# Agent attention and two feed-forward layers: the second layer moved one block further behind the first, and its weights decoded later

## The chip, the cores and the metric

The kernel runs on one core of a Trainium2 chip. The metric is the device time of one execution in microseconds (us); three runs of the kernel before gave a median of 1066.42 us. The engines are named as the profile names them: PE is TensorE, PEld its weight loads, ACT is ScalarE, DVE is VectorE, POOL is GpSimd, and SP is the engine whose queue issues all DMAs here.

## The reference

12480 tokens of width 128 attend through 49 agents, and the result passes two feed-forward layers with 2048 hidden columns. In the reference's words, cut to what is computed:

```
a2k = softmax(scale * agents @ k.T);  agent_v = a2k @ v          # 49 x 128
q2a = softmax(scale * q @ agents.T);  x = q2a @ agent_v          # 12480 x 128
h = x @ w_in1;  g = where(h >= 1, h, where(h <= -1, 0, (h + 1)**2 / 4));  y = g @ w_out1
h = y @ w_in2;  g = s * max(h, 0)**2 + b;                         out = g @ w_out2
```

The four weight matrices arrive as 64-bit floats and are decoded on the chip into a high and a low part (`fp32r`, a rounded fp32 that PE multiplies in one go).

## The kernel before, in words

**Before the first product.** All 13 groups of keys and then 13 groups of values are loaded by SP. PE forms the scores of the agents against the keys (`ks`), DVE finds their maxima, ACT takes exponentials (line 557, token `E`), PE turns them round (`st`), ACT or DVE copies them (`tok`, tokens `V`), and PE sums the values (`av`, tokens `a`). DVE divides (`avn`, token `n`), PE turns the result (`at`, token `T`), ACT and DVE split it (`avh`, `avl`, tokens `H`, `L`). Then PE multiplies it into the first layer's input weights (`aw`, tokens `W0` to `W3`), ACT rounds the product to `awh` (tokens `F`) and DVE keeps the rest in `awl` (tokens `G`). From then on the first layer works on the 49 attention weights of a token instead of its 128 values.

**Weights.** Each matrix comes in two pieces of 1 MB: B is `w_in1`, C is `w_out1`, D is `w_in2`, A is `w_out2`. A piece is decoded in eight steps, numbered 0 to 7; steps 1, 2 and 5 are on ACT (lines 381, 384, 399), the others on DVE (lines 376, 394, 389, 402, 407). `D0.1` is step 1 of piece D0. Three buffers hold raw pieces, so a load waits until step 7 of an earlier piece has freed one. The order of the loads on SP is the string `LOADS`; the order of everything else before the steady state is two strings of tokens, `SEQ` and `RAMP`, in which each engine runs its own tokens in the order written.

**Steps.** The tokens are cut into 25 blocks: one of 256, 23 of 512, one of 448. A block has eight steps of two hidden chunks each; step n belongs to block n // 8. In the first layer a step is `H` (products into PSUM), `R` and `S` (ACT: relu, square), `M` (DVE: cap), then a split into `gh` (token `c` on DVE or `g` on ACT) and `gl` (token `L`, DVE), and `O` (products into `y`). The first 12 steps are short: they skip the split, and `O` multiplies the fp32 values with fp32 weights (`w32`, built by tokens `U` from the decoded C). When a block of `y` is complete, ACT and DVE split it into `yh` and `yl`, and the second layer runs the same kind of step on it, in small letters: `h`, `r`, square, `G` or `c`, `l`, `o`. Three PSUM buffers of two banks take the results of `H`, `h`, the scores and the turned pieces.

**Steady state.** After the string `RAMP`, the function `steady` writes the steps two at a time by the table `PAIR`: step n of the first layer beside step n - D of the second. The lag D is one block and three steps, 11 steps. When the first layer is through, `TAIL` writes the rest of the second.

**Attention of the later blocks.** Blocks 3 and later get their attention weights in pairs of blocks. Pair v loads its queries, PE forms scores, DVE turns them into the tile `turned` (line 269), softmax follows there, DVE turns the packed result back into `turned` (line 284), and 32 DMAs (line 297) move it from `turned` into `pt` and `px`, from where `H` reads. Pair v is asked for at step 8 b - 17, where b is its first block; pair 0 at step 15.

Of the kernel before, what the change touches and what calls it, by code (L numbers as in the profile page):

```python
# [8 lines left out]
F32 = mybir.dt.float32  # L9
F32R = mybir.dt.float32r  # L10
# [8 lines left out]
def kernel(  # L19
# [18 lines left out]
    P = 128  # L38
# [11 lines left out]

    GR, XB, UB, WB, KV = 4, 3, 3, 2, 7
    WARM, CD = 10, 1
    PAT1, PAT2, TL = "11111101000001", "11011101", 11

# [6 lines left out]


    SEQ = (
# [8 lines left out]
    )  # L74
    VDVE = (0, 3, 4, 7, 8, 12)
    LOADS = (
        "k0 B0 k1 k2 k3 B1 k4 k5 k6 k7 k8 k12 k9 k10 k11 C0 v0 q0 D0 v1 C1 v2 v3 v4 v5 D1 v6 v7 v9 q1 v8 v10 v11 "
        "v12 A0 q2 A1"
    )
    RAMP = (  # L80
# [5 lines left out]
    )  # L86
    WORD = "B0 B1 C0 D0 C1 D1 A0 A1".split()
    NR, FP = 14, 12
    PAIR = {
        "PE": "H0 O0 o0 h0 O1 h1 o1 q1".split(),  # L90
        "ACT": "t0 R0 S0 G0 R1 S1 Y0 r0 Y1 t1 G1 r1".split(),
# [123 lines left out]
    def q_transpose(t):  # L215
        if t >= NB:
            return
        fill(len(fillers))
        w = blocks[t][1]
        tp = ps_h(f"tp{t}")[:, 0, :]  # L220
        for i, c0 in enumerate(subs(t)):
            nc.tensor.matmul(
                out=tp[:, c0:c0 + P], lhsT=ptok[t % NPT][:, i, :], rhs=ident_r,
                start=True, stop=True,
            )
        pt = pt_t[t] = ptp.tile([P, TB], F32R, tag="pt", name=f"pt{t}")
        if t >= QB:
            px = px_t[t] = late.tile([P, TB], F32R, tag="px", name=f"px{t}", bufs=3)

        def spread():  # L230
            nc.scalar.activation(out=pt[:, :w], in_=tp[:, :w], func=ACTF.Copy)
            if t < QB:
                return
            src = pt.bitcast(F32)
            for g in range(P // RG):
                nc.sync.dma_start(out=px.bitcast(F32)[g * RG:g * RG + XL, :w], in_=src[XN:NA, :w])

        qev.append(spread)
# [183 lines left out]
        )  # L422

    def sums_copy():
        cs.append(late.tile([P, TB], F32, tag="px", name="csum", bufs=3))
        nc.scalar.activation(out=cs[1], in_=cs[0], func=ACTF.Copy)

    def sums_turn():
# [28 lines left out]
    def agents_values(pro, dec, wi1h, wi1l):  # L457
# [157 lines left out]
            nc.vector.tensor_tensor(out=avl, in0=at[0], in1=avh.bitcast(F32), op=ALU.subtract)  # L615

        def weights(i):
            aw[i] = ps_h(f"aw{i}")[:, 0, :]
            ops = [(avh, wi1h), (avh, wi1l), (avl, wi1h)]
            for m, (a, w) in enumerate(ops):  # L620
                nc.tensor.matmul(
                    out=aw[i], lhsT=a, rhs=w[:, i * TB:(i + 1) * TB], start=(m == 0), stop=(m == len(ops) - 1)
                )
# [56 lines left out]
    JP = KF // 2  # L680
    NS = NB * JP
    D1, D2 = 2, 2
    D = JP + D1 + DX
    hp, gx, gh, gl = {}, {}, {}, {}
    y_ps, y_hl, o_ps = {}, {}, {}

# [17 lines left out]

    def fill_rows():

        extra["m"] = late.tile([P, DFF], F32R, name="awm")
        extra["x"] = late.tile([P, DFF // 4], F32R, name="awx")
        m, x, h, l = (w.bitcast(F32) for w in (extra["m"], extra["x"], awh, awl))
        for i, r in enumerate((0, LO)):  # L710
            nc.sync.dma_start(out=m[i * NA:(i + 1) * NA], in_=h[r:r + NA])
        nc.sync.dma_start(out=m[2 * NA:P], in_=l[0:XN])
        for g in range(P // RG):
            nc.sync.dma_start(
                out=x[g * RG:g * RG + XL].rearrange("p (q m) -> p q m", m=P),
                in_=l[XN:NA].rearrange("p (q g m) -> p q g m", g=4, m=P)[:, :, g, :],
            )
# [21 lines left out]
        return layer == 1 and n < FP  # L739

    def ring(kind, layer, n, dtype, bufs):
        pool = late if layer == 1 else extra["late2"]
        t = pool.tile([P, 2 * TB], dtype, tag=f"{kind}{layer}", name=f"{kind}{layer}_{n}", bufs=bufs)
        return t.rearrange("p (b n) -> p b n", b=2)

# [39 lines left out]

    def GH(layer, n):
        if layer == 1:
            return PAT1[n] if n < len(PAT1) else "0"
        return PAT2[n % len(PAT2)] if n < NS - TL else "0"

    def last_step(first):
# [40 lines left out]
    def evac(layer, part):  # L832
        if layer not in done:
            return
        t = done[layer]
        t0, w = blocks[t]
        o = o_ps[layer]
        if part == "h":
            yh = late.tile([P, TB], F32R, tag="yh", name=f"yh{t}", bufs=2)
            yl = late.tile([P, TB], F32R, tag="yl", name=f"yl{t}", bufs=2)  # L840
            y_hl[t] = (yh, yl)
            nc.scalar.activation(out=yh[:, :w], in_=o[:, :w], func=ACTF.Copy)
        elif part == "l":
            yh, yl = y_hl[t]
            nc.vector.tensor_tensor(out=yl[:, :w], in0=o[:, :w], in1=yh[:, :w].bitcast(F32), op=ALU.subtract)
            del done[1]
        else:
            osb = extra["late3"].tile([P, TB], F32, tag="osb", name=f"osb{t}", bufs=2)
            nc.vector.tensor_scalar(
                out=osb[:, :w], in0=o[:, :w], scalar1=s_sb[:, 0:1], scalar2=bcol[:, 0:1],  # L850
                op0=ALU.mult, op1=ALU.add,
            )
            nc.sync.dma_start(out=outT[:, t0:t0 + w], in_=osb[:, :w])
            del done[2]

    def ramp():
        does = {
            "H": lambda n: H(1, n), "R": lambda n: relu(1, n), "S": lambda n: square(1, n), "M": cap,
            "g": lambda n: hi(1, n, GH(1, n) == "1"), "L": lambda n: lo(1, n), "O": lambda n: O(1, n),
            "h": lambda n: H(2, n), "r": lambda n: relu(2, n), "s": lambda n: square(2, n),  # L860
            "G": lambda n: hi(2, n, GH(2, n) == "1"), "l": lambda n: lo(2, n), "o": lambda n: O(2, n),
            "Y": lambda: evac(1, "h"), "y": lambda: evac(1, "l"),
            "u": lambda n: pair_load(0), "q": extra["scores_q"], "p": q_transpose, "P": lambda n: q_evac(), "z": lambda k, i: zops[k][i](), "x": sums, "X": sums_copy, "B": sums_turn, "b": sums_keep,
            "U": wide,
        }
        for token in RAMP.split():
            if token[:2] in steps:
                piece_step(token[:2], int(token[3:]))
            elif token[0] == "=":
                extra[token[1]](int(token[2:]))  # L870
            elif token == "Q":
                extra["wide_end"].close()
                extra["late3"] = ctx.enter_context(tc.tile_pool(name="late3", bufs=1, reuse_waits="tile"))
                extra["t"] = extra["late3"].tile([P, QG * PKW], F32, name="turned")
            elif token == "K":
                fill_rows()
            elif token == "N":
                extra["dec_end"].close()
                extra["late2"] = ctx.enter_context(
                    tc.tile_pool(name="late2", bufs=1, side="right", reuse_waits="tile")  # L880
                )
            else:
                does[token[0]](*[int(x) for x in token[1:].split(".") if x])
            extra["pump"]()

    def steady():
# [9 lines left out]
                H(1, n + 1)  # L896

        slots = []
        at = {(8 * b[0] - 17 if v else NR + 1): v for v in range(NB) if (b := pair_blocks(v))}

        def turn(v):
            pair_turn(v)
# [118 lines left out]
```

## Time and profile before

| | before |
|---|---|
| median of three runs | 1066.42 us (1066.18 to 1067.35) |
| the profiled execution | 1066.61 us, span 1064.8 us from first to last instruction |
| PE busy | 1043.7 us, 98% of the span |
| ACT busy | 991.5 us, 93% |
| DVE busy | 974.4 us, 92% |
| first product of the first layer (H0) | 63.94 us after the span's start |

PE's busy time is modelled from pipelined instructions, and each of its records overlaps the next: what a product costs is read from the distance between two starts, not from a record's length.

### The profile page before, as it was taken

How to read it: one execution, taken by the hardware profiler on the slowest of the kernel's cores; microseconds unless marked ns; L12 is line 12 of the kernel's file. 1: busy time of each engine (PE TensorE's matmuls, PEld its weight loads, DVE VectorE, ACT ScalarE, POOL GpSimd, SP SyncE). 2: the span in 40 equal slices, each digit the busy share in tenths (PEclk: the TensorE clock that was granted, in tenths of full speed). 3: DMA queues.
4: the chain of work that ended last, by engine and by line, in shares of the span. 5: the costliest groups of instructions: out<-in, count | busy, mean ns of one | idle time of the engine just before them, and what ended most of it. 6: DMA issues, size and time to landing. Idle time of an engine off the chain costs nothing.

```text
span 1064.8 us, 13312 instructions
## 1 busy us (share of the span) xinstructions
PE 1043.7 (98%) x4931; PEld 793.2 (74%) x4931; DVE 974.4 (92%) x1115; ACT 991.5 (93%) x1070; POOL 0.9 (0%) x7
## 2 busy tenths in 40 slices
PE   7889999999999999999999999999999999999998
PEld 2677767777777777777777777777777777777787
DVE  6897989989999999999999999999999999999876
ACT  5988989999999999999999999999999999999986
POOL 0000000000000000000000000000000000000000
PEclk9899999999999999999999999999999999999999
DMA  9931020110010010010010020020020010010000
GB/s 357 391 120 31 24 59 10 29 42 10 20 50 11 19 51 11 18 52 10 16 54 10 13 58 10 12 59 11 11 57 11 11 40 10 9 40 10 1 11 19
DMA packets 32114, 47.68 MB, mean 45 GB/s; under 512 B 7285, under 2 KB 23653, under 8 KB 31409
## 3 DMA queue, kind: packets, MB, share of 16 engines
q1 hardware_dynamic: 32049, 46.83, 13.7%
q8 instruction: 39, 0.64, 0.2%
q14 instruction: 26, 0.21, 0.1%
HBM read 27.58 MB, written 6.39 MB: 32 GB/s over the span
## 4 chain that ended last, share of the span: by engine, by line
PE 87%; DVE 3%; ACT 2%; SPq 1%; DMA 1%; issue 1%; DVEq 0%; ACTq 0%
PE y L823 25%; PE h L700 25%; PE o L823 24%; PE h L730 8%; PE h L736 4%; SPq L297 1%; DVE gl L779 1%; DMA wu<-in_w_out 1%; PE qs L261 1%; DVE x L763 1%; ACT x L759 1%; DVE gh L774 0%; ACT gh L772 0%; ACT x L753 0%; ACT x L755 0%
## 5 line engine op out<-in xcount | busy, mean ns | idle before, releaser
L779 DVE TENSOR_TENSOR gl<-x,gh 128x1024 fp32r<-128x1024 f32 (+2 forms) x387 | 461.7, 1201 | 9.6 <-ACT gh L772 5.4
L759 ACT ACTIVATE x<-x 128x1024 f32<-128x1024 f32 (+2 forms) x387 | 405.8, 1049 | 11.4
L763 DVE SCALAR_TENSOR_TENSOR x<-h,x 128x1024 f32<-128x1024 f32 (+1 forms) x188 | 228.2, 1214 | 36.4 <-ACT x L759 36.1
L753 ACT ACTIVATE x<-h 128x1024 f32<-128x1024 f32 (+1 forms) x188 | 189.3, 1007 | 24.2 <-PE h L736 24.1
L755 ACT ACTIVATE x<-h 128x1024 f32<-128x1024 f32 (+2 forms) x199 | 197.1, 990 | 7.4 <-PE h L700 5.9
L774 DVE CAST gh<-x 128x1024 fp32r<-128x1024 f32 (+1 forms) x244 | 165.9, 681 | 15.6 <-ACT x L759 15.0
L823 PE MATMUL y<-gh,wo1h 128*128 128x512 f32 (+1 forms) x376 | 158.4, 421 | 0.0
L700 PE MATMUL h<-yh,wi2h 128*128 128x512 f32 (+2 forms) x400 | 156.6, 392 | 1.3 <-ACT x L755 1.1
L823 PE MATMUL o<-gh,wo2h 128*128 128x512 f32 (+2 forms) x400 | 156.3, 391 | 0.0
L700 PE MATMUL h<-yh,wi2l 128*128 128x512 f32 (+2 forms) x400 | 155.8, 390 | 0.0
L700 PE MATMUL h<-yl,wi2h 128*128 128x512 f32 (+2 forms) x400 | 155.4, 389 | 0.0
L823 PE MATMUL o<-gl,wo2h 128*128 128x512 f32 (+2 forms) x400 | 155.0, 387 | 0.2 <-DVE gl L779 0.2
L823 PE MATMUL o<-gh,wo2l 128*128 128x512 f32 (+2 forms) x400 | 155.0, 387 | 0.0
L772 ACT ACTIVATE gh<-x 128x1024 fp32r<-128x1024 f32 (+1 forms) x143 | 148.5, 1038 | 3.6 <-DVE x L763 0.5
L823 PE MATMUL y<-gl,wo1h 128*128 128x512 f32 (+1 forms) x376 | 148.1, 394 | 0.5 <-DVE gl L779 0.5
L823 PE MATMUL y<-gh,wo1l 128*128 128x512 f32 (+1 forms) x376 | 147.7, 393 | 0.0
L730 PE MATMUL h<-pt,awm 128*128 128x512 f32 (+1 forms) x368 | 100.7, 394 | 0.3 <-ACT x L755 0.3
L823 PEld LDWEIGHTS y<-gh,wo1h 128*128 128x128 f32 x376 | 70.6, 188 | 34.8 <-issue 17.2
L700 PEld LDWEIGHTS h<-yh,wi2h 128*128 128x128 f32 x400 | 75.2, 188 | 19.4 <-ACT x L755 2.0
L823 PEld LDWEIGHTS o<-gl,wo2h 128*128 128x128 f32 x400 | 75.1, 188 | 18.6 <-DVE gl L779 0.8
L700 PEld LDWEIGHTS h<-yl,wi2h 128*128 128x128 f32 x400 | 75.1, 188 | 17.5 <-issue 0.5
L823 PEld LDWEIGHTS o<-gh,wo2h 128*128 128x128 f32 x400 | 75.1, 188 | 16.7
(133 smaller groups left out, 881.2 us busy)
## 6 DMA issues: line engine op xcount, KB each, us to landing
k<-in_kT SPq DMA_DIRECT2D x12, 512.0 KB, 11.8
v<-in_v_main SPq DMA_DIRECT2D x12, 512.0 KB, 10.7
out_T<-osb SPq DMA_DIRECT2D x23, 256.0 KB, 2.0
pt<-turned SPq DMA_DIRECT2D x172, 32.0 KB, 1.8
px<-turned SPq DMA_DIRECT2D x172, 32.0 KB, 1.8
qbuf<-in_qT SPq DMA_DIRECT2D x10, 512.0 KB, 3.5
wu<-in_w_in SPq DMA_DIRECT2D x4, 1024.0 KB
wu<-in_w_out SPq DMA_DIRECT2D x4, 1024.0 KB, 8.5
```

What stands on the lines that cost most here:

```text
L261: nc.tensor.matmul(out=sc[j * RG:(j + 1) * RG, g], lhsT=a64[:, g * RG:(g + 1) * RG], rhs=qbuf[:, c0:c0 + QW].rearrange("p (b x) -> p b x", ...
L700: nc.tensor.matmul(out=h[:, i, :w], lhsT=a[:, sl], rhs=r, start=(m == 0), stop=(m == len(ops) - 1))
L730: nc.tensor.matmul(out=out[g], lhsT=awm[:, c * P:(c + 1) * P], rhs=pt_t[t][:, :w], start=True, stop=False)
L736: nc.tensor.matmul(out=out[g], lhsT=awx[r, q], rhs=px_t[t][r, :w], start=False, stop=True)
L753: nc.scalar.activation(out=x, in_=h, func=ACTF.Relu, scale=0.5, bias=0.5)
L755: nc.scalar.activation(out=x, in_=h, func=ACTF.Relu)
L759: nc.scalar.activation(out=x, in_=x, func=ACTF.Square)
L763: nc.vector.scalar_tensor_tensor(out=x, in0=h, scalar=1.0, in1=x, op0=ALU.max, op1=ALU.min)
L772: nc.scalar.activation(out=a, in_=x, func=ACTF.Copy)
L774: nc.vector.tensor_copy(out=a, in_=x)
L779: nc.vector.tensor_tensor(out=b, in0=x, in1=a.bitcast(F32), op=ALU.subtract)
L823: nc.tensor.matmul(out=o[:, :w], lhsT=l[:, c, :], rhs=r[:, i, :w], start=(c == 0 and m == 0), stop=(c == KF - 1 and m == len(ops) - 1),)
```

## The change

- The lag D of the second layer grows by one block (`LAG = 2`): 19 steps in place of 11. The string `RAMP` reaches to first-layer step 21 (`NR = 22`, before 14), and the tail has 19 steps of the second layer alone. The ring of `yh` and `yl` grows from two to three.
- The short steps are 20 in place of 12 (`FP`), so steps 12 to 19 are now short. Steps 20 and 21 put their `gh` on ACT (`PAT1`).
- The two pieces of `w_in2` are loaded behind the last values, with `w_out2` behind them. Their decoding moves accordingly: before, D is decoded among the values and half of A in front of H0; now D0 and all of A but nothing of C is decoded beside the first layer's steps.
- Pair 0 of the later blocks is worked off inside `RAMP` (tokens `j`, `J`, `f`), with `turned` in an earlier pool. Pair 1 is asked for at step 23, as before.
- `W0` and `W1` share one PSUM buffer, and `W2` and `W3` another.
- The second layer's `gl` gets a pool of its own where `w32` was, and the column sums of `w_out2` use another tile.
- `SEQ`, `LOADS`, `RAMP`, `WORD` and the list `VDVE` of copies on DVE are new strings.

```diff
-    PAT1, PAT2, TL = "11111101000001", "11011101", 11
+    PAT1, PAT2, TL = "11", "11011101", 19
...
-        "k0 B0 k1 k2 k3 B1 k4 k5 k6 k7 k8 k12 k9 k10 k11 C0 v0 q0 D0 v1 C1 v2 v3 v4 v5 D1 v6 v7 v9 q1 v8 v10 v11 "
-        "v12 A0 q2 A1"
+        "k0 B1 k1 k2 k3 k4 B0 k5 k6 k8 k7 k9 k10 k11 k12 v0 v1 q0 q1 C1 C0 v2 v3 v4 v5 v6 v7 v8 v9 v10 v11 v12 "
+        "D1 q2 D0 A0 A1"
...
-    WORD = "B0 B1 C0 D0 C1 D1 A0 A1".split()
-    NR, FP = 14, 12
+    WORD = "B1 B0 C0 C1 D1 D0 A0 A1".split()
+    NR, FP, LAG = 22, 20, 2
...
         def weights(i):
-            aw[i] = ps_h(f"aw{i}")[:, 0, :]
+            if i % 2 == 0:
+                aw["t"] = ps_h(f"aw{i}")
+            aw[i] = aw["t"][:, i % 2, :]
...
-    D = JP + D1 + DX
+    D = LAG * JP + D1 + DX
...
+        extra["t"] = late.tile([P, QG * PKW], F32, name="turned")
...
-        pool = late if layer == 1 else extra["late2"]
+        pool = late if layer == 1 else extra["late4" if kind == "gl" else "late2"]
...
-            return PAT1[n] if n < len(PAT1) else "0"
+            return PAT1[n - FP] if FP <= n < NR else "0"
...
+    def first_pair():
+        pair_turn(0)
+        zops["f"] = [op for i, op in enumerate(pair_steps(0)) if i != 3]
+
...
-        at = {(8 * b[0] - 17 if v else NR + 1): v for v in range(NB) if (b := pair_blocks(v))}
+        at = {8 * b[0] - 17: v for v in range(1, NB) if (b := pair_blocks(v))}
```

Three places of the order matter below. On ACT, the first stands around the roundings to `awh` (lines 626 and 628), before:

```order
L612 ACTIVATE avh<-at 128x128
L384 ACTIVATE wt<-wt,wbias 128x1024
L381 ACTIVATE wt<-wu 128x1024
L626 ACTIVATE awh<-aw_589 128x512
L626 ACTIVATE awh<-aw_593 128x512
```

and in the change:

```order
L574 ACTIVATE tok_522<-st_505 128x512
L381 ACTIVATE wt<-wu 128x1024
L384 ACTIVATE wt<-wt,wbias 128x1024
L231 ACTIVATE pt_549<-tp_546 128x256
L231 ACTIVATE pt_567<-tp_562 128x512
L612 ACTIVATE avh<-at 128x128
L381 ACTIVATE wt<-wu 128x1024
L399 ACTIVATE wi2h<-wt 128x1024
L628 ACTIVATE awh<-aw_579 128x512 x2
```

In both, a decoding step that reads a raw piece (`wu`) stands between `avh` and `awh`: `A1.1` before, `D0.1` now, and behind it now `D1.5`.

On DVE, the second place is the stretch from the end of pair 0 to the start of pair 1 in the change (before, the same two rows, line 284 and then line 269, stand 17 rows apart as well, with the second layer's rows 128x1024 wide):

```order
L284 STREAM_TRANSPOSE turned<-packed 128x8x5x32
L437 COPY bcol<-bcol 128x1
L766 SCALAR_TENSOR_TENSOR x_20_985<-h_20_971,x_20_985 128x1024
L782 TENSOR_TENSOR gl_0_1054<-x_0_927,gh_0_935 128x2x256
L782 TENSOR_TENSOR gl_1_1056<-x_1_933,gh_1_951 128x2x256
L766 SCALAR_TENSOR_TENSOR x_21_1028<-h_21_972,x_21_1028 128x1024
L782 TENSOR_TENSOR gl_20_1072<-x_20_985,gh_20_1067 128x1024
L777 CAST gh_2_1115<-x_2_1065 128x2x256
L782 TENSOR_TENSOR gl_21_1117<-x_21_1028,gh_21_1070 128x1024
L766 SCALAR_TENSOR_TENSOR x_22_1104<-h_22_1074,x_22_1104 128x1024
```

```order
L766 SCALAR_TENSOR_TENSOR x_23_1107<-h_23_1075,x_23_1107 128x1024
L782 TENSOR_TENSOR gl_22_1126<-x_22_1104,gh_22_1123 128x1024
L782 TENSOR_TENSOR gl_3_1128<-x_3_1110,gh_3_1113 128x2x256
L777 CAST gh_23_1130<-x_23_1107 128x1024
L269 STREAM_TRANSPOSE turned<-qs_1151 128x512
L302 TENSOR_REDUCE pm_1165<-turned 128x8
L303 TENSOR_TENSOR turned<-turned,pm_1165 128x8x49
L782 TENSOR_TENSOR gl_23_1169<-x_23_1107,gh_23_1130 128x1024
```

The turn of pair 1 (line 269) writes into `turned`, which the DMAs of pair 0 read; `gl` of step 23 is queued behind it, as it was before.

On SP, the third place is the end of the loads, before:

```order
L489 DMA v_433<-in_v_rest 64x128
L353 DMA wu<-in_w_out 128x8x256
L166 DMA qbuf<-in_qT 128x512
L353 DMA wu<-in_w_out 128x8x256
L510 DMA s_sb<-in_s 128x1
```

and in the change, where two loads of `w_in2` follow the last values:

```order
L489 DMA v_445<-in_v_rest 64x128
L351 DMA wu<-in_w_in 128x2048
L167 DMA qbuf<-in_qT 128x512
L351 DMA wu<-in_w_in 128x2048
L353 DMA wu<-in_w_out 128x8x256 x2
L510 DMA s_sb<-in_s 128x1
```

## Rows read from the trace of the kernel before

**Rows 1.** Windows: busy us of PE, PEld, DVE, ACT, POOL, PEclk, DMA share, GB/s

```profile
28.00:58.00 30.00, 25.86 (x269) 21.18 (x269) 25.67 (x45) 28.00 (x54) 0.00 (x0) 0.89 1.03 387
...
61.76:97.51 35.75, 34.19 (x168) 27.14 (x169) 29.94 (x45) 33.81 (x51) 0.00 (x0) 0.95 0.16 50
...
65.00:66.00 1.00, 0.87 (x5) 0.57 (x3) 1.00 (x3) 0.97 (x3) 0.00 (x0) 0.50 0.00 0
...
300.00:500.00 200.00, 200.00 (x920) 151.83 (x919) 187.48 (x207) 190.91 (x197) 0.00 (x0) 1.00 0.10 28
...
1035.00:1050.00 15.00, 15.00 (x72) 13.09 (x71) 12.21 (x15) 11.27 (x12) 0.00 (x0) 1.00 0.05 19
```

**Rows 2.** Chain that ended last, in order of time: start us, us, what

```profile
51.51 9.15 DMA wu<-in_w_out
...
145.40 1.88 DMA pt<-turned
...
161.83 1.40 PE h L700 x6
```

**Rows 3.** Timeline of PE, 84 to 87 us: start us, us, instruction

```profile
84.56 1.88 PE L823 MATMUL y<-gl,w 128*128 128x512 f32 x4
...
85.88 0.68 PE L700 MATMUL h<-yh,wi2h 128*128 128x256 f32 x1
86.39 0.28 PE L700 MATMUL h<-yl,wi2h 128*128 128x256 f32 x1
86.51 0.28 PE L700 MATMUL h<-yh,wi2l 128*128 128x256 f32 x1
```

**Rows 4.** Timeline of DVE and ACT from the maxima of the keys on

```profile
29.09 1.23 DVE L389 SCALAR_TENSOR_TENSOR wt<-wu,wt 128x1024 uint32<-128x1024 uint32 x1 [0.48 <-ACT wt L381]
...
30.60 0.72 ACT L557 ACTIVATE ST<-ST,nm 128x512 f32<-128x512 f32 x1 [0.18 <-DVE nm L553]
...
32.74 1.04 ACT L399 ACTIVATE wo1h<-wt 128x1024 fp32r<-128x1024 f32 x1
33.69 0.57 ACT L574 ACTIVATE tok<-st 128x512 f32<-128x512 f32 x1
...
39.07 1.14 ACT L381 ACTIVATE wt<-wu 128x1024 int32<-128x1024 uint32 x1
```

**Rows 5.** Timeline of SP, DVE and ACT in front of the first layer

```profile
50.41 0.39 SPq L353 DMA_DIRECT2D wu<-in_w_out  x1
...
56.38 1.14 ACT L381 ACTIVATE wt<-wu 128x1024 int32<-128x1024 uint32 x1 [0.48 <-DMA wu<-in_w_out]
...
56.84 0.34 DVE L601 TENSOR_SCALAR avn<-av,rden 128x128 f32<-128x128 f32 x1
...
60.74 1.12 ACT L381 ACTIVATE wt<-wu 128x1024 int32<-128x1024 uint32 x1 [1.50 <-DMA wu<-in_w_out]
...
61.76 1.57 ACT L626 ACTIVATE awh<-aw 128x512 fp32r<-128x512 f32 x3
```

**Rows 6.** Timeline of ACT: steps of 256 and of 512 tokens

```profile
69.63 0.58 ACT L753 ACTIVATE gl<-h 128x512 f32<-128x512 f32 x1
...
70.78 0.60 ACT L753 ACTIVATE gl<-h 128x512 f32<-128x512 f32 x1
...
126.52 1.01 ACT L753 ACTIVATE x<-h 128x1024 f32<-128x1024 f32 x1
...
128.53 1.01 ACT L755 ACTIVATE x<-h 128x1024 f32<-128x1024 f32 x1
```

**Rows 7.** Timeline of DVE and PE: pairs 0 and 1, step 23

```profile
127.58 1.51 DVE L284 STREAM_TRANSPOSE turned<-packed 128x1280 f32<-128x1280 f32 x1
...
147.40 0.72 DVE L269 STREAM_TRANSPOSE turned<-qs 128x512 f32<-128x512 f32 x1 [3.53 <-DMA pt<-turned]
...
149.23 1.22 DVE L779 TENSOR_TENSOR gl<-x,gh 128x1024 fp32r<-128x1024 f32 x1
...
150.50 0.50 PE L823 MATMUL y<-gl,wo1h 128*128 128x512 f32 x1 [0.21 <-DVE gl L779]
```

More of the change, by code (lines that the diff above doesn't have):

```diff
@@ L52 @@
     WARM, CD = 10, 1
-    PAT1, PAT2, TL = "11111101000001", "11011101", 11
+    PAT1, PAT2, TL = "11", "11011101", 19
     SEQ = (
[8 rows of a table removed]
[7 rows of a table added]
     )
-    VDVE = (0, 3, 4, 7, 8, 12)
+    VDVE = (4, 6, 7, 9, 12)
     LOADS = (
-        "k0 B0 k1 k2 k3 B1 k4 k5 k6 k7 k8 k12 k9 k10 k11 C0 v0 q0 D0 v1 C1 v2 v3 v4 v5 D1 v6 v7 v9 q1 v8 v10 v11 "
-        "v12 A0 q2 A1"
+        "k0 B1 k1 k2 k3 k4 B0 k5 k6 k8 k7 k9 k10 k11 k12 v0 v1 q0 q1 C1 C0 v2 v3 v4 v5 v6 v7 v8 v9 v10 v11 v12 "
+        "D1 q2 D0 A0 A1"
     )
     RAMP = (
[5 rows of a table removed]
-    )
-    WORD = "B0 B1 C0 D0 C1 D1 A0 A1".split()
-    NR, FP = 14, 12
[7 rows of a table added]
+    )
+    WORD = "B1 B0 C0 C1 D1 D0 A0 A1".split()
+    NR, FP, LAG = 22, 20, 2
     PAIR = {
@@ L217, in q_transpose @@
             return
-        fill(len(fillers))
         w = blocks[t][1]
@@ L424, in sums_copy @@
     def sums_copy():
-        cs.append(late.tile([P, TB], F32, tag="px", name="csum", bufs=3))
+        cs.append(ring("gh", 1, "sum", F32, GR)[:, 0, :])
         nc.scalar.activation(out=cs[1], in_=cs[0], func=ACTF.Copy)
@@ L838, in evac @@
         if part == "h":
-            yh = late.tile([P, TB], F32R, tag="yh", name=f"yh{t}", bufs=2)
-            yl = late.tile([P, TB], F32R, tag="yl", name=f"yl{t}", bufs=2)
+            yh = late.tile([P, TB], F32R, tag="yh", name=f"yh{t}", bufs=LAG + 1)
+            yl = late.tile([P, TB], F32R, tag="yl", name=f"yl{t}", bufs=LAG + 1)
             y_hl[t] = (yh, yl)
@@ L854, in evac @@
             del done[2]
+    def first_pair():
+        pair_turn(0)
+        zops["f"] = [op for i, op in enumerate(pair_steps(0)) if i != 3]
     def ramp():
         does = {
-            "H": lambda n: H(1, n), "R": lambda n: relu(1, n), "S": lambda n: square(1, n), "M": cap,
+            "H": lambda n: H(1, n) if n < QB * JP else H1_pair(n), "j": lambda: pair_scores(0), "J": first_pair,
+            "f": lambda i: zops["f"][i](), "R": lambda n: relu(1, n), "S": lambda n: square(1, n), "M": cap,
             "g": lambda n: hi(1, n, GH(1, n) == "1"), "L": lambda n: lo(1, n), "O": lambda n: O(1, n),
@@ L873, in ramp @@
                 extra["late3"] = ctx.enter_context(tc.tile_pool(name="late3", bufs=1, reuse_waits="tile"))
-                extra["t"] = extra["late3"].tile([P, QG * PKW], F32, name="turned")
+                extra["late4"] = ctx.enter_context(
+                    tc.tile_pool(name="late4", bufs=1, side="right", reuse_waits="tile")
+                )
             elif token == "K":
```

27 rows, old and new, of tables (RAMP, SEQ) are left out of this document.

## The prediction

> **What bounds the kernel now.** I read the windows first. From 300 to 500 us PE is busy for all 200 us, ACT for 191 and DVE for 187; from 1035 to 1050, where the second layer runs alone, PE is busy for all 15 while ACT and DVE have a fifth to a quarter free [rows 1]. The chain of waits says the same at finer grain: six products of 512 columns take 1.40 us, one behind the other [rows 2], and neighbours of 256 columns start 0.12 us apart, 0.70 for six [rows 3]. So behind the ramp PE sets the time, and nothing that the change does there alters the number of its products: the extra eight steps of the tail are taken out of the paired stretch, and PE is full in both. The result is decided by when PE becomes full.
>
> Ahead of that stand two other stretches. From 28 to 58 us ACT is busy for 28 of 30 us and the DMA queues carry 387 GB/s without a pause [rows 1]: the values, their exponentials and the decoding of C and D. From the first rounding to `awh` at 61.76 to step 14's relu at 97.51, ACT is busy for 33.81 of 35.75 us, 5.4% idle [rows 1]. The front of the first layer is thus a queue of work on ACT, with PE nearly full beside it.
>
> **A fixed point to count from.** Both kernels reach step 23's `O`, whose third product waits for `gl` of step 23; before, it starts at 150.50 [rows 7]. The first layer stands equal there. The second stands eight steps further back after the change: `h` at step 5 in place of 13, `o` at 3 in place of 11. What PE has still to do is more by h6 to h13 (2 x 0.70 + 6 x 1.40 = 9.8) and o4 to o11 (4 x 0.70 + 4 x 1.40 = 8.4), 18.2 us. So the change breaks even if that product starts at 150.5 - 18.2 = **132.3**.
>
> **The start, earlier by 5 us.** *Exponentials.* Before, a decoding step of C (DVE, 1.23 us) stands between the maxima and the first exponential at 30.60, with another of 0.6 ahead of it [rows 4]. Without them I put the first at 29.0. *ACT's queue from there* to the last copy of the turned values: 12 exponentials of 0.72 and a last short pair of 0.95 (9.6); 8 copies of 0.48, since a record overlaps the next by 0.1 as line 399's 1.04 against 0.95 shows (3.8); two pieces of C with three steps each of 1.05, 1.05 and 0.95 (6.2); four small operations for the queries (1.2). Sum 20.8, to 49.8 [rows 4]. Before, D's steps stood there too; they are what the change takes out. *Behind it*, `avn` on DVE is queued behind `D1.3`, which waits for `D1.1` on ACT: 1.1 + 1.15, to 52.1. From `avn` to the end of `avh` took 1.2 (56.84 to 58.0) [rows 5]; I take 1.5 for the two copies to `pt` in front of it: 53.6. *Then a wait that replaces one.* Before, `A1.1` stood in front of the `awh` roundings and waited for its load until 60.74; the load took 9.15 us [rows 2, 5], and `awh` began at 61.76. Now `D0.1` stands there and waits for D0, whose buffer comes free with C's last step on DVE, about 48.8. The nearest row is A0, issued at 50.41 and read at 56.38, 6.0 us in a queue with some values still ahead [rows 5]. So D0 is there at 54.8; `D0.1` and `D1.5` take 2.1, and `awh` begins at **56.9**. Bounds: 55.7 if D0 doesn't wait at all (53.6 + 2.1), 60.0 with A1's 9.15.
>
> **The ramp on ACT, to the end of pair 0.** In front of step 20 ACT has: four roundings (2.0), eight steps of 256 at 1.15 and twelve of 512 at 1.97 (9.2 + 23.6; 2.01 where a square follows its relu at once [rows 6], a little less where two relus follow each other), eight decoding steps of D0 and A (8.2), `pt`, `yh` twice, the queries, pair 0 and the sums (3.2), and two layer-two steps of 256 with their `gh` (3.4). Sum 49.6. With ACT idle for 5.4%, as in the ramp before, that is 52.4; its bounds are 49.6 with no idle and 55.6 with twice as much. Then DVE caps step 19, makes the last part of pair 0 and turns it: 1.2 + 0.5 + 1.5 [rows 7], less overlaps 3.0. Pair 0 ends at 56.9 + 52.4 + 3.0 = **112.3**.
>
> **The short steps** lie in this stretch. Four records of an fp32 product pair start 1.32 us ahead of the next product, which itself is late: 84.56 to 86.39, less one product of 0.12, is 1.71 us for a short step's `O` of 512 columns [rows 3], against 1.40 for six fp32r products. Eight more cost PE 2.5 us and spare DVE a difference of 1.2 and one engine a copy each. I set them at nothing, since ACT's 52 us hide PE's 44 or so there (20 `H` 14.3, eight `O` of 256 at 0.86, ten of 512 at 1.71, sums, scores and two `h` 5); without that cover they cost 2.5. The Trainium skill, "FP8 and Floating Point Precision", section "TensorE Precision Notes", has it that a true fp32 product takes four passes through the array; two products would be eight passes against six, and at 0.233 us a pass an estimate of 1.87 in place of 1.71, 3.7 us for the eight steps; the trace's 1.71 decides.
>
> **The wait behind pair 0.** Before, pair 1's turn waited 3.53 us for pair 0's DMAs to have read `turned`: pair 0 ended at 129.09 and the last read landed at 145.40 + 1.88 = 147.28, 18.2 us later; the turn began at 147.40 and `gl` of step 23, queued behind it, ended at 150.4, PE's product at 150.50: 21.4 us behind pair 0's end [rows 2, 7]. These DMAs go one after the other on SP and are the same after the change. Between the two turns DVE has 15 rows, ten of them as before or narrower, and PE has 13 us of products from H22 on: both less than 18.2. So the wait stays and grows, and step 23's product starts at 112.3 + 21.2 = **133.5** (0.2 less: `gl` follows the same three rows). Before, the second layer's steps there were 512 wide and gave PE products to go on with; now they are 256 wide, half the work.
>
> Behind the wait DVE owes M24, l4, c24, M25, yl and L24 (four of about 1.15 or 0.6, 5.2 us), and PE has 4.3 us of products ahead of step 24's last part: 0.9 more.
>
> **Sum.** 133.5 - 132.3 + 0.9 = +2.1 us with these middle values. I move it down by 0.5, as D0's load has less ahead of it in the queue than A0 had, whose 1 MB followed values not yet landed: +1.6. The profiled execution took 1066.6, so 1068.2; it lay 0.2 above the median, so **1068.0**, +0.15%. A measurement of this kernel can tell about 0.2% (2.1 us) from no change, so 1064.3 to 1068.5 is "the same". What the early start gains (4.9) goes to D's and A's decoding, which lay under the loads and now takes its turn in ACT's ramp, and to the wait for `turned`.
>
> **Rivals.** *(a) The middle values hold:* 1066 to 1070, chance 0.46. *(b) Slower: D0's load.* If it takes A1's 9.15 us, `awh` begins at 60.0 and all behind it moves by 3.1: 1071.1. It decides from a landing at 56 us on. For it: `D0.1` stands ahead of `awh` in ACT's order; against: no values are still to come when D0 is issued. 0.16. *(c) Slower: the clock.* Behind the wait for the last raw piece and the roundings to `awh` from 61.76 on [rows 5], the granted clock was 0.50, the 1.2 GHz level, from 65 to 66 [rows 1]. The wait for `turned` leaves PE idle for some 4 us in the middle of the run; if the clock falls, some 3 us of products take twice their time, 1.4 more: 1069.4. Against: the 3.53 us wait before brought no fall, as PE had products. 0.14. The Trainium skill, "TensorE: Matmul & The Clock Gate", section "HAM oscillation — how this bites in real kernels", says that a gap in the products brings the throttled level back for those behind it; by that rule (c) happens, and the trace agrees for the one gap it shows. *(d) Faster: ACT's ramp has no idle time and D0 is there in time:* 1.2 + 2.8 less, 1064.0; the order of tokens was written for the new ramp, but its own trace would have to show no wait on ACT. 0.14. *(e) Faster: the turn doesn't hold PE up,* since pair 0 ends earlier or PE has products to go on with: then PE's products from H22 (some 115) bound step 23 at 128.5, 4 earlier and no debt: 1063.5. 0.10.
>
> Faster by over 0.2%: (d) and (e), less a part that ends inside, 0.21. Slower: (b), most of (c), and the upper third of (a), 0.38. The same: 0.41. The range for 8 in 10 runs from (e) and (d) to just above (b): 1063.4 to 1071.8.
>
> **What would show it.** Right: the first exponential near 29, `awh` near 57 behind a line 381 that waits for a load; ACT busy for about 95% from there to step 19; line 269's second run waiting 4 to 6 us for `pt<-turned`; PE idle near 130 and full from about 140. Wrong: ACT waiting in front of `awh` until 58 or more (b); a granted clock of 0.50 near 133 (c); PE already full at 115 (e). A tail in which PE has gaps would make the whole count wrong, since the eight steps moved there would then cost more than they save.

## The result and the profile after

| | before | after |
|---|---|---|
| median of four runs | 1066.82 us (1066.18 to 1067.35) | 1075.42 us (1073.96 to 1076.78) |
| ratio, with 95% interval | | 1.0077 [1.0065, 1.0089] |
| profiled execution, its span | 1066.61 us, 1064.8 us | 1076.34 us, 1074.6 us |
| PE, ACT, DVE busy | 98%, 93%, 92% | 98%, 92%, 90% |

The change made the kernel 0.77% slower, against a forecast of +0.15% with a range up to 1071.8. The four runs after are two pairs: 1076.34 and 1076.78 us with a mean granted clock of 0.986 and 0.987 over the span, 1074.51 and 1073.96 us with 0.992 and 0.993.

**Where the count ends.** The rounding of a finished block of `y` to `yh` is a mark that both kernels have. The timeline of ACT shows it for block 3 and for the last block, block 24 (start us, us, instruction; a wait in brackets), in the kernel before:

```profile
191.77 0.59 ACT L842 ACTIVATE yh<-y 128x512 fp32r<-128x512 f32 x1
...
1033.20 0.55 ACT L842 ACTIVATE yh<-y 128x448 fp32r<-128x448 f32 x1 [2.10 <-PE y L823]
```

and in the changed one:

```profile
28.84 0.72 ACT L557 ACTIVATE ST<-ST,nm 128x512 f32<-128x512 f32 x1 [2.19 <-DVE nm L553]
...
55.73 1.16 ACT L381 ACTIVATE wt<-wu 128x1024 int32<-128x1024 uint32 x1
...
57.75 1.69 ACT L628 ACTIVATE awh<-aw 128x512 fp32r<-128x512 f32 x3
...
179.26 0.59 ACT L845 ACTIVATE yh<-y 128x512 fp32r<-128x512 f32 x1
...
1020.69 0.55 ACT L845 ACTIVATE yh<-y 128x448 fp32r<-128x448 f32 x1 [2.10 <-PE y L826]
```

The changed kernel is 12.51 us ahead at block 3 and 12.51 us ahead at block 24: in 840 us of paired steps not a hundredth is won or lost. From the last `yh` to the end of the span it takes 53.9 us, before 31.6: the eight extra steps of the second layer alone cost 22.3. So 22.3 us had to be won ahead of block 3, and 12.5 were. The loss, 9.8 us in the two profiled executions, lies in front of 180 us.

**The stretch that should have brought it.** Windows over the ramp, from the first `awh` to the square of step 19, over the three stretches of low clock, and over the two stretches of [rows 1] further back (busy us of PE, PEld, DVE, ACT, POOL, then PEclk, DMA share, GB/s):

```profile
57.75:115.84 58.09, 53.47 (x214) 34.35 (x212) 43.58 (x60) 48.30 (x66) 0.00 (x0) 0.91 0.19 61
62.00:69.00 7.00, 5.82 (x21) 5.19 (x21) 7.00 (x10) 6.11 (x12) 0.00 (x0) 0.53 0.67 238
100.00:103.00 3.00, 3.00 (x4) 1.19 (x4) 1.51 (x2) 1.99 (x2) 0.00 (x0) 0.50 0.00 0
138.00:144.00 6.00, 5.77 (x20) 4.84 (x21) 5.93 (x9) 1.89 (x4) 0.00 (x0) 0.50 0.42 115
300.00:500.00 200.00, 200.00 (x910) 152.46 (x909) 188.02 (x208) 192.18 (x198) 0.00 (x0) 1.00 0.08 23
1035.00:1050.00 15.00, 15.00 (x68) 12.27 (x67) 10.29 (x11) 11.07 (x12) 0.00 (x0) 1.00 0.01 2
```

ACT was busy for 48.30 us of the ramp's 58.09; it stood idle for 9.8 us, 17%, where the ramp before had 5.4% [rows 1]. PE is as full as before in the steady state and in the tail. Who was waited for, on ACT in the ramp and on PE from 56 to 300 us (us in total, times, the longest):

```profile
ACT yh L845 <- PE y L826: 3.2, 1, 3.2
ACT gl L756 <- PE h L739: 2.5, 2, 1.9
ACT x L758 <- PE h L702: 1.8, 1, 1.8
ACT gl L756 <- PE h L702: 1.7, 2, 0.8
```

```profile
PE h L702 <- DVE turned L269: 2.7, 1, 2.7
PE h L702 <- DVE awl L632: 1.9, 1, 1.9
PE h L739 <- DMA px<-pt: 1.8, 2, 1.2
```

ACT waited for PE, and PE in its turn had waited three times: for `awl` and for `px` in the ramp, for `turned` behind it. The timeline of PE shows the first, and the second with what followed:

```profile
63.19 0.58 PE L702 MATMUL h<-pt,awh 128*128 128x256 f32 x1 [1.93 <-DVE awl L632]
...
95.22 1.49 PE L733 MATMUL h<-pt,awm 128*128 128x512 f32 x4
96.64 0.49 PE L739 MATMUL h<-px,awx 19*128 19x512 f32 x2
97.75 0.49 PE L739 MATMUL h<-px,awx 19*128 19x512 f32 x1 [0.62 <-DMA px<-pt]
99.40 0.47 PE L739 MATMUL h<-px,awx 19*128 19x512 f32 x1 [1.16 <-DMA px<-pt]
99.80 5.40 PE L826 MATMUL y<-gl,w 128*128 128x512 f32 x8
...
105.60 1.07 PE L261 MATMUL qs<-qbuf,a 128*32 128x256 f32 x16
...
138.23 0.58 PE L702 MATMUL h<-yh,wi2h 128*128 128x256 f32 x1 [2.72 <-DVE turned L269]
...
140.56 0.80 PE L826 MATMUL y<-gl,wo1h 128*128 128x512 f32 x1
```

Block 2's weights are turned and copied behind step 14's `H`; the DMAs from `pt` to `px` follow, and the chain of waits gives the last of them 6.76 us to land:

```profile
90.54 0.67 SPq L236
...
92.51 6.76 DMA px<-pt
...
99.87 5.33 PE y L826 x8
```

Step 16's `H` stands on it. In the kernel before, the same four DMAs were issued earlier against their use:

```profile
94.85 2.54 SPq L236 DMA_DIRECT2D px<-pt  x4
...
106.08 0.51 PE L736 MATMUL h<-px,awx 19*128 19x512 f32 x4
```

Queued behind step 16's `H` on PE in the changed kernel are O14, O15, two column sums and pair 0's scores. The eight fp32 records of O14 and O15 took 5.40 us, and the clock was 0.50 from 100 to 103; four such records took 1.88 at full clock [rows 3]. Pair 0's scores came at 105.60, its turn back ended at 117.61 + 1.51 = 119.12, and from there on everything went as forecast, on DVE:

```profile
117.61 1.51 DVE L284 STREAM_TRANSPOSE turned<-packed 128x1280 f32<-128x1280 f32 x1
...
137.46 0.72 DVE L269 STREAM_TRANSPOSE turned<-qs 128x512 f32<-128x512 f32 x1 [4.97 <-DMA pt<-turned]
...
139.29 1.22 DVE L782 TENSOR_TENSOR gl<-x,gh 128x1024 fp32r<-128x1024 f32 x1
```

Step 23's third product started at 140.56, 21.4 us behind pair 0's end; before it was 150.50, and also 21.4 [rows 7].

### The profile page after: what moved, and what is told of

It reads as the page before. It is cut to its first block, busy times and chain, and to the rows that moved or that the text cites. A ratio compares the mean times of both kernels' runs of the same rounds, so it can differ in the third digit from the quotient of the medians.

```text
span 1074.6 us, 13266 instructions
## 1 busy us (share of the span) xinstructions
PE 1052.8 (98%) x4914; PEld 795.8 (74%) x4914; DVE 965.1 (90%) x1103; ACT 986.1 (92%) x1066; POOL 0.9 (0%) x7
## 4 chain that ended last, share of the span: by engine, by line
PE 90%; ACT 4%; DVE 3%; SPq 2%; DMA 1%; issue 1%; DVEq 0%; ACTq 0%
PE y L826 26%; PE h L702 25%; PE o L826 25%; PE h L733 8%; PE h L739 4%; SPq L297 1%; PE qs L261 1%; DVE mxs L540 1%; DMA px<-pt 1%; PE warm L656 1%; ACT gl L756 1%; ACT gl L762 1%; DMA wu<-in_w_in 0%; ACT ST L557 0%; ACT wt L381 0%
## 5 line engine op out<-in xcount | busy, mean ns | idle before, releaser
L782 DVE TENSOR_TENSOR gl<-x,gh 128x1024 fp32r<-128x1024 f32 (+2 forms) x379 | 452.2, 1201 | 10.1 <-ACT gh L775 5.3
L762 ACT ACTIVATE x<-x 128x1024 f32<-128x1024 f32 (+2 forms) x379 | 397.3, 1048 | 11.2
L766 DVE SCALAR_TENSOR_TENSOR x<-h,x 128x1024 f32<-128x1024 f32 (+1 forms) x180 | 218.5, 1214 | 35.7 <-ACT x L762 35.5
L756 ACT ACTIVATE x<-h 128x1024 f32<-128x1024 f32 (+1 forms) x180 | 181.2, 1006 | 22.0 <-PE h L739 21.9
L777 DVE CAST gh<-x 128x1024 fp32r<-128x1024 f32 (+2 forms) x241 | 164.0, 681 | 21.2 <-ACT x L762 20.6
L826 PE MATMUL y<-gh,wo1h 128*128 128x512 f32 (+1 forms) x360 | 152.2, 423 | 0.0
L775 ACT ACTIVATE gh<-x 128x1024 fp32r<-128x1024 f32 (+1 forms) x138 | 143.1, 1037 | 3.1 <-DVE x L766 0.2
L826 PE MATMUL y<-gl,wo1h 128*128 128x512 f32 (+1 forms) x360 | 142.4, 396 | 0.4 <-DVE gl L782 0.2
L826 PE MATMUL y<-gh,wo1l 128*128 128x512 f32 (+1 forms) x360 | 141.9, 394 | 0.0
L702 PEld LDWEIGHTS h<-yh,wi2l 128*128 128x128 f32 x400 | 75.7, 189 | 16.5
```

What stands on the lines that cost most here:

```text
L702: nc.tensor.matmul(out=h[:, i, :w], lhsT=a[:, sl], rhs=r, start=(m == 0), stop=(m == len(ops) - 1))
L756: nc.scalar.activation(out=x, in_=h, func=ACTF.Relu, scale=0.5, bias=0.5)
L762: nc.scalar.activation(out=x, in_=x, func=ACTF.Square)
L766: nc.vector.scalar_tensor_tensor(out=x, in0=h, scalar=1.0, in1=x, op0=ALU.max, op1=ALU.min)
L775: nc.scalar.activation(out=a, in_=x, func=ACTF.Copy)
L777: nc.vector.tensor_copy(out=a, in_=x)
```

## The experiments

The theory after the traces: PE waited at three places for a buffer or a tile that comes late in the new order; each wait costs its length and, where the clock falls behind it, slow products as well; all of it ends in pair 0 and step 23. The rivals: ACT's queue was simply longer than I had counted and the waits lie under it; the short steps' fp32 products hold PE; the clock alone. The first three edits are aimed at one wait each, by order and not by dropping a dependency; the fourth has all three. A ratio is always to the kernel before on the same chip; a difference in us is one of medians, and as runs of one kernel lie up to 5 us apart, the size of a single step is known to 1 or 2 us only.

**The first wait.** Step 2's `H` waited for the PSUM buffer that `W2` and `W3` share, until the last `awl` had been read from it.

```diff
-        "=F2 =G1 q2 u3 z2.0 z2.1 z2.2 H0 =G2 D0.2 R0 U0 =F3 H1 S0 R1 S1 =G3 z2.3 K M0 H2 ..."
+        "=F2 =F3 =G1 q2 u3 =G2 =G3 z2.0 z2.1 z2.2 H0 D0.2 R0 U0 H1 S0 R1 S1 z2.3 K M0 H2 ..."
```

> Edit: the last two roundings to awh and the last two rests in awl (tokens =F3, =G2, =G3) are written ahead of block 2's softmax pieces, D0.2 and the first U. Theory (waits on PE in front of late buffers, each with a fall of the granted clock behind it): step 2's H, which started at 63.19 because its PSUM buffer was free only when the last awl had been taken, starts near 61.5, the clock stays at 1.00 or falls later, ACT's two idle stretches of 0.8 us near 67 and 69 go, and 2 us are saved: 1073.4. Rival (ACT's queue alone sets the ramp, the awl work is only moved on DVE): under 0.5 us, 1075.

Measured: 1074.16 us (1073.33 to 1076.11), ratio 1.0078 [1.0065, 1.0091]. The median is 1.3 us lower, but the ranges overlap, and the interval is that of the changed kernel itself; by its time alone it is not shown to be worth anything. Its trace says why it is no clean removal. Step 2's `H` starts at 61.43 as expected, but step 3's then waits for step 0's cap (line 766), and starts at 63.83 in place of 64.20; what differs behind it is the granted clock, 1.00 in place of 0.53 (a row of PE's timeline, and a window as above):

```profile
63.83 0.39 PE L702 MATMUL h<-pt,awh 128*128 128x256 f32 x1 [1.66 <-DVE gl L766]
...
62.00:69.00 7.00, 4.82 (x27) 3.64 (x26) 7.00 (x10) 6.66 (x13) 0.00 (x0) 1.00 0.64 220
```

So the edit moved the wait by one step and kept the clock up.

**The second wait.**

```diff
-        ... S9 A1.6 O8 R10 M9 R11 S10 M10 H12 ... H14 p2 O11 P2 M13 ...
+        ... S9 A1.6 O8 p2 R10 M9 R11 S10 P2 M10 H12 ... H14 O11 M13 ...
```

> Edit: block 2's attention weights are turned and copied behind step 11's H in place of step 14's (tokens p2, P2), so that the four DMAs from pt to px are issued some 6 us earlier. Theory: step 16's H no longer waits for px (1.8 us, last product at 99.40), PE goes on with O14 and O15 from about 97 without the fall to 0.50 at 100 to 103, pair 0's scores come near 101 to 102 in place of 105.60, and step 23's third product comes 4 to 5 us earlier: 1070.9. Rival (ACT, with its steps, is what pair 0 waits for, and px is hidden beside it): under 1 us, 1075. Second rival (the clock alone, not the wait): 1.5 us.

Measured: 1070.67 us (1070.21 to 1073.23), ratio 1.0046 [1.0034, 1.0058]: the median is 4.8 us less, as the theory had it, and 3.3 us by the two ratios (1.0046 against 1.0077, their intervals apart), from a wait of 1.8 us. Its list of PE's waits has no `px` any more; the other two are there:

```profile
PE h L702 <- DVE turned L269: 3.3, 1, 3.3
PE h L702 <- DVE awl L632: 1.9, 1, 1.9
```

The granted clock was 1.00 from 96 to 104 in this run, so the gain holds the wait and the slow products together. The rival that the wait lies under ACT's queue falls.

**The third wait.**

```diff
-        at = {8 * b[0] - 17: v for v in range(1, NB) if (b := pair_blocks(v))}
+        at = {8 * b[0] - (15 if v == 1 else 17): v for v in range(1, NB) if (b := pair_blocks(v))}
```

> Edit: pair 1 is asked for two steps later, at step 25 in place of 23, so that its turn stands behind the moment at which pair 0's DMAs have read the tile turned (137.4). Theory: gl of step 23 is no longer queued behind that wait, PE goes on at 135.4 and the clock doesn't fall at 138: step 23's third product at 136.5 to 137 in place of 140.56 and 3 to 4 us saved: 1071.9. Rival (DVE and ACT owe the same work anyway, so that PE only waits a little later): under 1 us, 1075. Rival on the other side: pair 1's moves end too late for step 40 and the time is longer than 1076.

Measured: 1072.07 us (1069.8 to 1075.22), ratio 1.0050 [1.0037, 1.0063]: 3.4 us less by the medians. `gl` of step 23 no longer stood behind the turn. The wait moved on to pair 2's turn, which waited 3.1 us for pair 1's reads, and from 170 to 300 us PE waited for nothing behind it.

**All three.**

> Edit: the three edits together. Theory: they add up, as each removes a wait at a place of its own: 2 + 4.5 + 3.5 = 10 us, 1065.4, no slower than the kernel before. Rival (one queue sets the time behind all three): no better than the best of them alone, 1071.

Measured: 1066.81 us (1065.56 to 1068.43, 11 runs), ratio 1.0000 [0.9991, 1.0008]. Together the three are worth 8.6 us by the medians, and the change is then worth nothing, for better or worse. Its windows over the same ramp (57.40 is its first `awh`, 110.32 the end of step 19's square) and over the two later stretches:

```profile
57.40:110.32 52.92, 48.41 (x212) 30.56 (x210) 43.18 (x60) 47.94 (x66) 0.00 (x0) 1.00 0.21 67
100.00:103.00 3.00, 3.00 (x31) 2.27 (x31) 2.74 (x4) 1.60 (x4) 0.00 (x0) 1.00 0.27 57
130.00:144.00 14.00, 13.69 (x87) 9.85 (x86) 13.87 (x19) 12.99 (x19) 0.00 (x0) 1.00 0.22 61
```

The ramp takes 52.9 us, near the 52.4 of the forecast, but by another sum: ACT has 47.9 us of work and is idle for 5.0 (9.4%), where the forecast had 49.6 and 2.8. In single executions the same stretch takes 58.1 us in the changed kernel, 54.8 with the first edit, 54.4 with the second, 58.4 with the third, which touches nothing there, and 52.9 with all: the first two are what brings the ramp back.

```profile
168.69 0.59 ACT L845 ACTIVATE yh<-y 128x512 fp32r<-128x512 f32 x1
```

Block 3's `yh` is 23.1 us ahead of the kernel before, just above the 22.3 that the tail takes; 0.9 of them are lost by block 5 (250.16 against 272.38, 22.2 ahead). The single edits have it at 176.23, 175.90 and 175.04, which is 3.0, 3.4 and 4.2 us ahead of the changed kernel, 10.6 in sum and 10.6 with all three: the gains add up.

**The same late pair in the kernel before.**

> Edit, on the kernel before: pair 1 asked for at step 25 in place of 23. There DVE's turn waited 3.53 us, but PE only 0.21 us behind it. Theory (a wait costs what PE loses by it): within 0.5 us of the kernel before, 1066.5 to 1067.5. Rival (DVE's lost 3.5 us are a debt that PE pays later): 3 us faster, 1064. Rival on the other side (pair 1's moves, now later, hold up pair 2's turn at step 39, as in the kernel with all three edits, where it waited 3.7 us): 0.5 to 1 us slower.

Measured: 1066.69 us, ratio 0.9995 [0.9986, 1.0004]: the same. DVE's wait of 3.5 us there costs nothing, as PE waited 0.21 us behind it; in the changed kernel PE waited 2.7, and the edit at the same place brought 3.4. That the second layer's products, 512 columns wide there and 256 here, make the difference is not tested apart; it fits that pair 2's turn in the third edit, with products 512 wide about it, waited 3.1 us and held PE for nothing.

**The clock apart from the waits.** Products with zeros fill PE's gaps in front of the three places; what is computed stays the same, and so do the waits' causes. The core of the edit:

```diff
+        for _ in range(count):
+            nc.tensor.matmul(out=out[0:LO], lhsT=zl, rhs=rhs, start=alone, stop=alone)
...
+        if n == 16:
+            hold(12, out[0], pt_t[t])
```

> Edit, on the changed kernel: products with a matrix of zeros, 64 columns wide, are added in PE's three gaps (8 of 512 columns in front of step 2's H, 12 between the two parts of step 16's H, 11 in front of the second layer's step 5), into a free PSUM buffer or adding zero to an open one. All waits stay as they are; only PE isn't idle in them. Theory (each wait costs its own length and, behind it, products at 1.2 GHz): the granted clock stays at 1.00 at 62 to 69, 100 to 103 and 138 to 144, and 1.7 + 1.6 + 1.5 to 3 us come back: 1070 to 1071. Rival (the waits alone are the loss, and the slow products lie in time that PE has anyway): under 1 us, 1075.

Measured: 1072.09 us (1071.0 to 1073.09), ratio 1.0045 [1.0031, 1.0058]: 3.3 us less. The windows over the three stretches:

```profile
62.00:69.00 7.00, 6.39 (x36) 5.18 (x36) 7.00 (x12) 6.70 (x13) 0.00 (x0) 1.00 0.57 204
96.00:103.00 7.00, 7.00 (x40) 3.39 (x39) 2.77 (x3) 4.54 (x5) 0.00 (x0) 1.00 0.00 0
130.00:144.00 14.00, 12.45 (x72) 9.16 (x71) 11.26 (x15) 10.46 (x15) 0.00 (x0) 1.00 0.23 63
```

The clock stayed at 2.4 GHz throughout, while DVE's turn of pair 1 still waited 4.5 us. So about 3.3 of the 8.6 us go back to slow products, and some 5 are left for the waits themselves. The parting is not clean: in the profiled execution the first `awh` is already 1.2 us earlier (56.55), for which the edit gives no reason, and the wait for `px` can't be seen, since the twelve products lie in it (from 93.86 to the products of `px` at 96.74).

**The short steps.** Twelve in place of 20; the splits of steps 12 to 19 (tokens g, L) stand right behind their caps.

```diff
-    PAT1, PAT2, TL = "11", "11011101", 19
+    PAT1, PAT2, TL = "0000000011", "11011101", 19
-    NR, FP, LAG = 22, 20, 2
+    NR, FP, LAG = 22, 12, 2
...
-        ... M12 ... M13 ...
+        ... M12 g12 L12 ... M13 g13 L13 ...
```

> Edit, on the changed kernel: 12 short steps in place of 20 (FP = 12), so that steps 12 to 19 are split by DVE and multiplied in three fp32r products. Theory (PE has room in the ramp and DVE gains by the short steps): the same or slower, 1075.4 to 1077.5. Rival (the fp32 products of steps 12 to 19, 0.31 us more each on PE, are part of the loss): 2.5 us faster, 1073.

Measured: 1079.55 us (1079.09 to 1080.58), ratio 1.0114 [1.0100, 1.0128]: 4.1 us slower than the changed kernel. Over the same 58.09 us as above, DVE was busy for 53.36 (43.58 with 20 short steps):

```profile
57.75:115.84 58.09, 49.63 (x216) 34.30 (x214) 53.36 (x70) 46.70 (x65) 0.00 (x0) 0.91 0.18 61
```

and PE waited 4.4 us for its caps. So the rival falls: the fp32 products cost less than the splits on DVE that take their place. What they cost by themselves this run doesn't show, and another place for the splits was not tried.

**What sets the ramp.** First 3.0 us more on ACT:

```diff
+            for _ in range(2 if n in (9, 11, 13) else 1):
                 nc.scalar.activation(out=x, in_=h, func=ACTF.Relu, scale=0.5, bias=0.5)
```

> Edit, on the changed kernel: the relu of steps 9, 11 and 13 is done twice (the same values again), 3.0 us more on ACT between 78 and 89. Theory of the prediction (ACT's queue sets the ramp): pair 0 and all behind it move by 3 us, 1078.4. Rival (PE's queue sets it there, with fp32 products, and ACT has room): under 1 us, 1076. Between the two, if each sets part of it: 1077.

Measured: 1077.87 us (1075.97 to 1080.19), ratio 1.0093 [1.0077, 1.0109], 2.4 us slower by the medians, with an interval that overlaps the changed kernel's. Then 2.8 us more on PE:

```diff
+        if layer == 1 and n in (9, 10, 11):
+            hold(4, o)
```

> Edit, on the changed kernel: four products with zeros behind each of O9, O10 and O11 (64 columns of zeros, 512 columns, added to the open y), 12 x 0.23 = 2.8 us more on PE between 86 and 92. Theory of the prediction (ACT sets the ramp, PE's products are hidden): under 0.5 us, 1075.8. Rival (PE is full from 82 to 96, so that the ramp is PE's as much as ACT's): 2 to 2.8 us slower, 1077.8.

Measured: 1074.53 us (1074.17 to 1076.53), ratio 1.0071 [1.0058, 1.0083]: not slower. The times alone leave the first of the two open; the ramps in the traces don't: from the first `awh` to the end of step 19's square it is 61.7 us with more on ACT, 57.7 with more on PE, and 58.1 in the changed kernel. At these places ACT sets the ramp, and PE's products are hidden.

**Two attempts at more.** The first puts step 16's `H` ahead of O13 on PE.

```diff
-        ... N M14 x0 S15 M15 O13 H16 R16 ...
+        ... N M14 S15 M15 H16 x0 O13 R16 ...
```

> Edit, on the kernel with all three edits: step 16's H is written ahead of O13 and of the first column sums on PE; pair 1's pieces are taken two per step up to step 34, so that its moves end before pair 2's turn; and =F3, =G2, =G3 stand behind the copy of block 2's scores. Theory: ACT's 2.4 us in front of step 16's relu and the 0.9 us lost between blocks 2 and 5 come back in part, 1 to 2 us faster than with the three edits: 1065.3. Rival (PE's products, not ACT, set the ramp from step 12 on): the same, 1066.8.

Measured: 1069.75 us (1068.35 to 1070.88), ratio 1.0022 [1.0013, 1.0031], 2.9 us slower than with the three edits, and both expectations miss. One new wait is in its list, where PE stood before the cap of step 14 with O13 queued behind it:

```profile
PE h L733 <- DVE gl L766: 1.4, 1, 1.4
```

The run also changed the order of the roundings to `awh`, and how much that had in it stays open; pair 1's pieces, taken two per step, are in the second attempt too. That one leaves the roundings alone:

```diff
-        ... M14 x0 S15 M15 O13 H16 R16 O14 O15 x1 S16 M16 R17 S17 x2 j Y M17 h0 x3 x4 J h1 ...
+        ... M14 S15 M15 O13 H16 x0 R16 O14 O15 j S16 M16 R17 x1 S17 J x2 Y M17 h0 x3 x4 h1 ...
-                        add(("F", n), [], fill, 2 if n < Q1 * JP else 1)
+                        add(("F", n), [], fill, 2 if n < Q1 * JP + 10 else 1)
```

> Edit, on the kernel with all three edits: the first column sums go behind step 16's H, pair 0's scores ahead of the next column sums and its turn ahead of the cap of step 17, and pair 1's pieces are taken two per step up to step 34. Theory (pair 0's end still sets step 23, and PE is what step 16 and pair 0's scores wait for): pair 0 ends 1 to 2 us earlier and 0.9 us between blocks 2 and 5 come back: 1065, the first one below the kernel before. Rival (behind the removed waits PE has no gap left that pair 0 decides): the same as with the three edits, 1066.8.

Measured: 1066.86 us (1066.45 to 1067.81), ratio 0.9999 [0.9991, 1.0008]: the rival's number. The rival's reason holds as well: pair 0 ends 56.2 us behind the first `awh` in this run and in that with the three edits. No version was found that beats the kernel before.

## Why the prediction was wrong, step by step

- *The count from a fixed point: right to 1 or 2 us.* Step 23's product at 140.56 is 8.3 us behind the break-even of 132.3; the profiled execution came out 9.7 slower, so 1.5 in place of 0.9 was still owed behind it. With the three edits the product is at 129.88, 2.4 us ahead of break-even, yet the time is that of before: there 2.4 us are owed.
- *The start: right in its number, partly by luck.* The first exponential at 28.84 (29.0); `awh` at 57.75 (56.9, within its bounds). Two errors stand against each other in it. `avh` ended at 55.69 and not at 53.6: ACT's queue, added up without a gap, stood idle for 1.8 us between 30 and 36, waiting for PE's scores and turned values, and `avn` started at 54.46 in place of 52.1, behind decoding steps of DVE that began at 52.71. And the wait of 1.2 for D0's load did not come: line 381 at 55.73 has none in front, so rival (b) fell.
- *The ramp: the step that failed.* "With ACT idle for 5.4%, as in the ramp before, that is 52.4; its bounds are 49.6 with no idle and 55.6 with twice as much." The work was right (48.3 us measured, 49.6 counted) and so was the engine (3.0 us more on ACT made the ramp 3.6 longer, 2.8 more on PE did not). The idle share was taken over from another order. In the new one PE waited for `awl` and for `px`, and ACT waited for PE behind that: 9.8 us idle, 58.1 in all, beyond the upper bound. The wait for `px` is new. One for `awl` the old order had too, of 2.7 us in front of its last products of `aw`; in the new one it stands in front of step 2, and the first edit shows that little of its length is won back by removing it (step 3's `H` comes 0.4 us earlier); the clock behind it is. Both places could be found in the order and the trace before together: the shared PSUM buffer is in the diff, and the DMAs from `pt` to `px`, issued behind step 14 in the new order up to 92.5, were wanted at 96.6, 4 us later, where before they had 9 (the last issued at 96.8, first used at 106.1). I listed the waits that the change named, and not those of tiles whose reader had moved.
- *The last part of pair 0 and the wait behind it: right.* 3.3 us from step 19's square to pair 0's end (3.0 forecast), then 21.4 (21.2); the turn waited 4.97 us (4 to 6).
- *The short steps: right that PE's products are hidden, as far as the 2.8 us more on PE show; wrong in setting the exchange at nothing.* Against twelve short steps, with the splits on DVE, it is worth 4.1 us. PE had less room than counted: with the three edits the profile has it busy for 48.4 of 52.9 us at full clock, where the forecast had 44 or so in 52.
- *The clock, rival (c): it happened, at three places from the ramp on.* (Ahead of the ramp it was low in both kernels, 0.52 from 28 to 34 us, and 0.70 before.) It had 0.14 and 1.4 us, for one place; keeping the clock up at all three gave 3.3 us back. The Trainium skill, "TensorE: Matmul & The Clock Gate", section "HAM oscillation — how this bites in real kernels", says that a wait of PE that is long enough brings the throttled level back for the products behind it; the changed kernel's profile agrees at all three gaps (1.9, 1.8 and 2.7 us, then 0.53, 0.50 and 0.50). With the first edit alone the gaps in front of step 3 (1.7 us) and of `px` (1.8 us, from 95 to 98) brought no fall, at 1.00 throughout, so what tells the one from the other stays open.
- *The sum.* Later than forecast: `awh` 0.9, the ramp 5.7, pair 0's last part and the wait 0.5, the debt 0.6, and the 0.5 that I had taken off: 8.2 in all, against 1076.34 - 1068.2 = 8.1 measured. One price among the rivals was added up wrongly: in (e), 133.5 less 128.5 is 5.0 and not 4, which with the 0.9 gives some 1062 in place of 1063.5. Nothing here hangs on it.

## What to carry to other kernels

When a schedule is re-ordered, an idle share measured in the old order is no estimate for the new one: go through each tile whose producer and reader have both moved, small DMAs between tiles and shared PSUM buffers above all, and compare the distance between them with the latency in the trace. A wait on a full PE can cost its length, the products that run at half clock behind it, and whatever is queued behind it and starts a chain of its own: here the removal of one of 1.8 us was worth 3.3 to 4.8. Whether a wait goes or only moves on by a step is read from the next trace, as with `awl`. A lag that fills the start is paid back in the tail step for step, and the count at one mark in the steady state (22.3 us needed, 12.5 won) tells it without any experiment.

## What the runs showed of the hardware that was not expected

- Four DMAs of 38 KB each from one SBUF tile to another, 19 rows of 2 KB, took 2.5 us to issue, and the last landed 6.76 us behind its issue, beside idle DMA queues (share 0.03 to 0.07 from 94 to 100 us).
- With products of a stationary tile of 64 columns of zeros in gaps of 2 to 3 us, PE's granted clock was 1.00 at all three places, and the kernel 3.3 us faster, though they compute nothing.
- The mean granted clock of one program differed from run to run, 0.986 to 0.993 over the four runs of the changed kernel; and a gap of 1.8 us in front of the same products was followed by the lower clock there (0.50 from 100 to 103) and by none with the first edit (1.00 from 94 to 104).
